# Key-value sums of a linear-attention and expert kernel in five visits instead of nine, with 17 stationary columns, and the placing products in two

## The chip, the core and the metric

The kernel runs on one core of a Trainium2 chip. The metric is the device time of one execution in microseconds (us), and the median of several runs is compared. TensorE is called PE here, and its weight loads PEld; VectorE is DVE, ScalarE is ACT, GpSimd is POOL and SyncE is SP.

## The reference, cut to what matters

A layer norm of `x` (2048 tokens of 512) feeds two branches, and both are added to `x`. The first branch is linear attention with 32 heads of 16: keys and queries go through a small matrix per head and two softmaxes, and the sums over all tokens of key features times values are what the queries are multiplied with. The second is a mixture of eight experts of which each token uses two.

```python
phi_k = concat([softmax(pk), softmax(-pk)])          # 2048 x 32 heads x 32
kv  = einsum("bhsf,bhsd->bhfd", phi_k, v)            # sums over the tokens
z   = einsum("bhsf->bhf", phi_k)
num = einsum("bhqf,bhfd->bhqd", phi_q, kv)
o   = num / (einsum("bhqf,bhf->bhq", phi_q, z)[..., None] + 1e-6)
att = o @ wo
gates = softmax(xn @ wg); top 2 of 8, normalised
out = x + att + sum_e cw[:, e] * (gelu(xn @ w1[e]) @ w2[e])
```

## The kernel before

The 2048 tokens are 16 tiles of 128, in four chunks of four tiles. An opening stretch (to about 162 us) makes the layer norm, the projections and the routing; then eight experts follow, each in 14 steps of 128 hidden columns, 112 steps in all. Nearly every product is taken three times (`mm3`, L174 to L176: high by high, high by low, low by high, of float32r halves), with 128 stationary columns and 496 or 512 moving ones in the opening stretch and 240 to 512 in the experts.

What each function of the opening stretch does, for token tile `t` or chunk `c`:

- `transp(t)` turns the normed tile on PE (L326, four transposes) and splits it: ACT makes the high half (L341), DVE the low half (L342).
- `proj_k(t)`, `proj_v(t)` and `proj_q(c, b)` are the projections, twelve matmuls each. ACT copies the result out (L429 and L430, L361, L479).
- `k_sub(t)` (DVE, L439 to L442), `k_exp(t)` (ACT, L449) and `k_norm(t)` (DVE, L454 to L456) make the key features of a tile in place.
- `kv(t)` (L501) adds a tile's key features times values to a bank of PSUM: 32 float32 matmuls, one for each head, with 18 stationary columns (16 of the values, then two of ones, which POOL fills at L357) and 32 moving columns; head `4b+c` lands in partitions `32c` and up. PE carries each of them out as two records, so that one `kv` is 64 matmul records and 64 weight loads. A tile's feature tile and value tile come free behind it.
- `kv_take(part)` adds a bank's sums to `kb` on DVE (L1080), and `kv_turn` turns them. Of a head's rows only the 16 of the values and the first one of ones (`t[:, :, 16]`) are read later.
- `one_hot(t)` (DVE, L648 and L649) makes two tokens tiles' slot matrices of the routing, and `place(t)` (L658) multiplies them on PE, four float16 matmuls of 144 columns. `route_index` (from L666) reads the sum, and the first expert's tokens are gathered from it.

A visit is a run of one kind of small matmul between the large ones. The order of PE, SP, ACT and DVE is the order of the code: nothing is reordered on these four engines. POOL's instructions are placed by a scheduler. In the opening stretch the `kv` visits stand at L892 (tiles 0 and 1), L901 (2 and 3), L916 (4 and 5) and L1015 (6 and 7). Later work is handed to the experts' steps by a table: `at(s, f, t)` puts `f(t)` behind the first layer and ahead of the second layer of step `s`. There the visits are: tiles 8 and 9 in step 5, 10 and 11 in step 7, 12 and 13 in step 13, 14 in step 20 and 15 in step 21. That makes nine. Memory is handed out by lists (`slot`, `free`), the longest free first in most places, so that another order gives other tiles to the same work.

## Time and profile before

| what | value |
|---|---|
| median of 3 runs | 861.32 us (861.12 to 864.41) |
| the profiled execution's own time | 861.69 us |
| its span, first to last instruction | 859.4 us |
| PE busy | 853.4 us, 99% of the span, 5889 matmul records |
| DVE, ACT and POOL busy | 661.7, 439.1 and 170.7 us |

The page of the profile gives these shares for the whole execution; what single pieces cost is read from the timelines of the engines, which list instructions with their start, duration and number. A matmul's duration there overlaps the next one's, so that the distance from start to start is what counts. `[1.63 <-ACT xTh L341]` behind a row says how long the engine stood idle before it and who ended that.

### The profile page before, as it was taken

What the parts mean: (1) busy time and instruction counts of PE and PEld (TensorE: products, weight loads), DVE (VectorE), ACT (ScalarE), POOL (GpSimd) and SP (SyncE); (2) the same over time, 40 slices, a digit from 0 to 9 for tenths busy, and PEclk for the clock granted to TensorE, in tenths of its full rate; (3) what the DMA queues carried; (4) which work ended last, traced back from release to release, by engine and by line L of the source; (5) the groups of instructions that cost most, each with busy time, mean ns of one, the idle gap of its engine ahead of it and who ended that gap; (6) DMA issues with size and microseconds to landing.
All of it is one profiled execution on the core that took longest, in us unless ns stands there. A gap on an engine that the chain in (4) does not pass through costs nothing.

```text
span 859.4 us, 15983 instructions
## 1 busy us (share of the span) xinstructions
PE 853.4 (99%) x5889; PEld 767.7 (89%) x5889; DVE 661.7 (77%) x1092; ACT 439.1 (51%) x723; POOL 170.7 (20%) x240
## 2 busy tenths in 40 slices
PE   9999999999999999999999999999999999999998
PEld 8888888899999999999999999998877888788886
DVE  6889899888783478878788877978778988755952
ACT  4453522743734364566556665456575566433541
POOL 5000002010004112411241141116421422200011
PEclk9999999999999999999999999999999999999999
DMA  8220106573317341833364257435642735678633
GB/s 296 99 98 2 50 14 191 163 226 100 123 61 223 129 135 47 257 120 110 105 206 134 88 164 191 145 110 165 210 151 83 236 115 187 215 291 248 211 109 101
DMA packets 123399, 126.99 MB, mean 148 GB/s; under 512 B 12342, under 2 KB 87606, under 8 KB 123312
## 3 DMA queue, kind: packets, MB, share of 16 engines
q1 hardware_dynamic: 115408, 106.10, 38.9%
q0 software_dynamic: 7088, 19.36, 7.0%
q8 instruction: 48, 0.79, 0.4%
q10 hardware_dynamic: 816, 0.43, 0.2%
q14 instruction: 39, 0.32, 0.1%
HBM read 98.62 MB, written 27.25 MB: 146 GB/s over the span
## 4 chain that ended last, share of the span: by engine, by line
PE 98%; DVE 1%; DMA 0%; issue 0%; DVEq 0%
PE pH L174 12%; PE pH L175 12%; PE pH L176 12%; PE pY L1259 9%; PE pY L1336 6%; PE pY L1337 6%; PE pY L1342 6%; PE pY L1302 4%; PE pY L1338 2%; PE pY L1339 2%; PE pY L1344 2%; PE pV L174 2%; PE pK L174 2%; PE pQ L474 2%; PE pV L176 2%; PE pO L176 2%
## 5 line engine op out<-in xcount | busy, mean ns | idle before, releaser
L1213 ACT ACTIVATE gl<-pH 128x276 f32<-128x276 f32 (+6 forms) x182 | 77.5, 435 | 242.5 <-PE pH L176 242.3
L1218 DVE TENSOR_TENSOR h<-gl,h 128x512 fp32r<-128x512 f32 (+6 forms) x112 | 78.2, 698 | 98.0 <-ACT h L1215 96.6
L1226 POOL DMA_INDIRECT y_rows<-keptN,pidx x68 | 72.5, 1066 | 235.2 <-ACT gl L1213 200.8
L176 PE MATMUL pH<-keptR,ws 128*128 128x258 f32 (+3 forms) x276 | 82.7, 300 | 0.0
L174 PE MATMUL pH<-keptR,ws 128*128 128x270 f32 (+3 forms) x240 | 72.5, 302 | 0.0
L175 PE MATMUL pH<-keptR,ws 128*128 128x270 f32 (+3 forms) x240 | 72.4, 302 | 0.0
L1215 ACT CAST h<-gl 128x512 fp32r<-128x512 f32 (+6 forms) x112 | 70.5, 629 | 3.5
L175 PE MATMUL pH<-xgl,ws 128*128 128x260 f32 (+3 forms) x204 | 64.6, 317 | 0.0
L174 PE MATMUL pH<-xgh,ws 128*128 128x260 f32 (+3 forms) x204 | 64.6, 316 | 0.0
L1337 PE MATMUL pY<-h,ws 128*128 128x388 f32 (+4 forms) x180 | 62.4, 347 | 0.0
L276 ACT CAST keptR<-keptN 128x1024 fp32r<-128x1024 f32 (+4 forms) x75 | 50.6, 705 | 20.9 <-DVE keptN L996 8.7
L276 ACT CAST ws<-keptN 128x1024 fp32r<-128x1024 f32 x55 | 57.6, 1047 | 7.1 <-PE pY L1259 7.1
L176 PE MATMUL pH<-xgh,ws 128*128 128x272 f32 (+3 forms) x188 | 59.2, 315 | 0.0
L1336 PE MATMUL pY<-h,ws 128*128 128x416 f32 (+4 forms) x168 | 58.5, 348 | 0.0
L1259 PE MATMUL pY<-ws,h 128*128 128x512 f32 x216 | 56.0, 391 | 0.0
L279 DVE TENSOR_TENSOR ws<-keptN,ws 128x1024 fp32r<-128x1024 f32 x36 | 43.5, 1210 | 13.1 <-ACT ws L276 13.0
L176 PEld LDWEIGHTS pH<-keptR,ws 128*128 128x128 f32 x276 | 52.1, 189 | 1.3
L971 POOL DMA_INDIRECT keptN<-xn_rows,tidx x30 | 33.0, 1101 | 97.3 <-DVE vv L675 47.0
L1259 PEld LDWEIGHTS pY<-ws,h 128*128 128x128 f32 x216 | 40.3, 188 | 10.1 <-ACT gl L1213 2.1
L175 PEld LDWEIGHTS pH<-keptR,ws 128*128 128x128 f32 x240 | 45.3, 189 | 2.3
L176 PE MATMUL pH<-xgh,keptR 128*128 128x272 f32 (+3 forms) x148 | 47.1, 318 | 0.0
L174 PEld LDWEIGHTS pH<-keptR,ws 128*128 128x128 f32 x240 | 45.1, 188 | 1.3
(340 smaller groups left out, 2406.0 us busy)
## 6 DMA issues: line engine op xcount, KB each, us to landing
keptN<-in_B_w_dram SPq DMA_DIRECT2D x172, 256.0 KB, 3.8
wr<-in_B_w_dram SPq DMA_DIRECT2D x52, 256.0 KB, 4.1
keptN<-y_rows SPq DMA_DIRECT2D x16, 512.0 KB, 6.0
x_slots<-keptN SPq DMA_DIRECT2D x25, 256.0 KB, 4.7
keptN<-in_A_x_dram SPq DMA_DIRECT2D x16, 256.0 KB, 4.8
xn_rows<-keptN SPq DMA_DIRECT2D x16, 256.0 KB, 2.6
keptN<-x_slots SPq DMA_DIRECT2D x32, 128.0 KB, 4.4
keptN<-in_A_x_dram SPq DMA_DIRECT2D x8, 512.0 KB, 4.5
```

What stands on the lines that cost most here:

```text
L174: nc.tensor.matmul(ps, lh, rh, start=(i == 0), stop=False)
L175: nc.tensor.matmul(ps, lh, rl, start=False, stop=False)
L176: nc.tensor.matmul(ps, ll, rh, start=False, stop=(i == n - 1))
L276: nc.scalar.copy(dst_h, src)
L1213: step[:] = [nc.scalar.activation(g[:, c:c + m], ps[:, :m], AF.Gelu_apprx_tanh)]
L1215: nc.scalar.copy(h[:, 0:full], g)
L1218: nc.vector.tensor_sub(h[:, xw:], g, f32(h[:, 0:full]))
L1226: i = nc.gpsimd.indirect_dma_start(out=to, out_offset=bass.IndirectOffsetOnAxis(ap=rows, axis=0), in_=y, in_offset=None)
L1259: nc.tensor.matmul(yb[e][i], ht[r][:, o:o + P], wsp[r][z][:, D:], start=(b == 0 and low + z == 0), stop=(r % FB == FB - 1 and low > 0))
L1336: nc.tensor.matmul(ps[i][:, 0:w - P], vh, h[:, P:w], start=st, stop=False, skip_group_check=True)
L1337: nc.tensor.matmul(ps[i][:, 0:m], vl, h[:, P:cap], start=False, stop=False, skip_group_check=True)
L1342: nc.tensor.matmul(ps[i][:, 0:m], v[0][:, i * P:(i + 1) * P], h[:, gw + P:], start=False, stop=sp_, skip_group_check=True)
```

## The change

- A `kv` matmul has 17 stationary columns: one column of ones instead of two. `kv_take` reads 17 rows of each head group.
- In the opening stretch `kv(0)` to `kv(3)` are one visit behind `proj_k(8)` to `proj_k(11)`, directly ahead of the transposes of tiles 12 to 15, and `kv(4)` to `kv(7)` are one visit where tiles 6 and 7 were.
- `proj_k(6)` and `proj_k(7)` go ahead of the transposes of tiles 8 to 11, with `k_norm(2)`; `proj_q(0, 3)` goes directly behind the other three of its chunk and ahead of `proj_k(8)`.
- In the experts tiles 8 to 11 are one visit in step 5, and 14 and 15 one visit in step 21. The nine visits become five.
- `place` is called for eight pairs of tiles in two visits of four calls instead of four visits of two.

```diff
-                nc.tensor.matmul(kvp[part][32 * c:32 * c + 18, b * 32:(b + 1) * 32],
-                                 vt[t // 2][:, t % 2, n, :], e[:, n * 32:(n + 1) * 32],
+                nc.tensor.matmul(kvp[part][32 * c:32 * c + 17, b * 32:(b + 1) * 32],
+                                 vt[t // 2][:, t % 2, n, 0:17], e[:, n * 32:(n + 1) * 32],
...
     k_norm(1)
+    proj_k(6)
+    k_norm(2)
+    proj_k(7)
     for t in range(8, 12):
         transp(t)
-    k_norm(2)
-    proj_k(6)
     k_norm(3)
     k_sub(4)
-    proj_k(7)
     k_sub(5)
 
-    for b in range(3):
+    for b in range(4):
         proj_q(0, b)
-    kv(0)
-    kv(1)
     k_exp(4, 5)
...
     k_sub(6)
-    proj_k(8)
-    kv(2)
-    kv(3)
-    proj_k(9)
-    proj_k(10)
-    proj_k(11)
-    proj_q(0, 3)
+    for t in range(8, 12):
+        proj_k(t)
+    for t in range(4):
+        kv(t)
     for t in range(12, 16):
         transp(t)
...
-    kv(4)
-    kv(5)
     proj_k(15)
...
-    kv(6)
-    kv(7)
+    for t in range(4, 8):
+        kv(t)
...
-        if t > 0:
-            place(t - 4)
-            place(t - 2)
+        if t in (8, 16):
+            for u in range(t - 8, t, 2):
+                place(u)
...
-            o, i = (z[32 * c:32 * c + 18] for z in (kb, ps))
+            o, i = (z[32 * c:32 * c + 17] for z in (kb, ps))
...
-        at((t | 1) - 4 if t < 12 else 13 if t < 14 else t + 6, kv, t)
+        at(5 if t < 12 else 13 if t < 14 else 21, kv, t)
```

On PE, the place where tiles 2 and 3 were summed between two key projections before (`pK` is a projection's bank, `kv` the bank of the sums, `pT` one of transposes):

```order
L175 MATMUL pK_1022<-wfl_254,xTh_794 128x496
L176 MATMUL pK_1022<-wfh_253,xTl_796 128x496
L501 MATMUL kv_924<-keptN_80,keptN_86 18x32 x32
L501 MATMUL kv_924<-keptN_84,keptN_86 18x32 x32
L174 MATMUL pK_1102<-wfh_208,xTh_793 128x496
L175 MATMUL pK_1102<-wfl_209,xTh_793 128x496
```

The same sums on PE in the change, behind the projection of tile 11:

```order
L176 MATMUL pK_1018<-wfh_253,xTl_831 128x496
L501 MATMUL kv_1033<-keptN_75,keptN_85 17x32 x32
L501 MATMUL kv_1033<-keptN_76,keptN_85 17x32 x32
L501 MATMUL kv_1033<-keptN_80,keptN_86 17x32 x32
L501 MATMUL kv_1033<-keptN_84,keptN_86 17x32 x32
L326 MATMUL pT_1166<-ident,keptN_78 128x128 x4
L326 MATMUL pT_1175<-ident,keptN_79 128x128 x4
L326 MATMUL pT_1184<-ident,keptN_74 128x128 x4
L326 MATMUL pT_1193<-ident,keptN_82 128x128 x4
L174 MATMUL pK_1217<-wfh_208,xTh_1162 128x496
```

Tiles 0 and 1, which had a visit of their own behind three query projections, and tiles 2 and 3 now stand together, and the transposes follow without a large matmul between.

On PE, behind the first query projection of the second chunk, before:

```order
L475 MATMUL pQ_1380<-keptR_96,wfl_405 128x512
L476 MATMUL pQ_1380<-keptR_98,wfh_404 128x512
L501 MATMUL kv_924<-keptN_76,keptN_89 18x32 x32
L501 MATMUL kv_924<-keptN_80,keptN_89 18x32 x32
L474 MATMUL pQ_1458<-keptR_95,wfh_388 128x512
L475 MATMUL pQ_1458<-keptR_95,wfl_389 128x512
```

and in the change:

```order
L475 MATMUL pQ_1316<-keptR_96,wfl_405 128x512
L476 MATMUL pQ_1316<-keptR_98,wfh_404 128x512
L501 MATMUL kv_1033<-keptN_73,keptN_88 17x32 x32
L501 MATMUL kv_1033<-keptN_71,keptN_88 17x32 x32
L501 MATMUL kv_1033<-keptN_72,keptN_89 17x32 x32
L501 MATMUL kv_1033<-keptN_75,keptN_89 17x32 x32
L474 MATMUL pQ_1458<-keptR_95,wfh_388 128x512
L475 MATMUL pQ_1458<-keptR_95,wfl_389 128x512
```

Tiles 4 and 5 came down from between two key projections; tiles 6 and 7, the last of the four now, stand where they stood.

On ACT, the copies of the query projections and the exponentials of tiles 4 and 5 behind them, as the difference of the two orders:

```order
 L479 COPY keptN_81<-pQ_882 128x512
 L479 COPY keptN_81<-pQ_896 128x512
 L479 COPY keptN_77<-pQ_910 128x512
+L479 COPY keptN_77<-pQ_924 128x512
 L449 ACTIVATE keptN_73<-keptN_73 128x1024
 L449 ACTIVATE keptN_71<-keptN_71 128x1024
```

The fourth query projection's copy now stands ahead of the two exponentials; before it stood behind the copies of tiles 8 to 11.

## Rows read from the trace of the kernel before

**Rows 1.** The page: busy time, share and instructions of each engine, and the shares of the chain that ended last.

```profile
PE 853.4 (99%) x5889; PEld 767.7 (89%) x5889; DVE 661.7 (77%) x1092; ACT 439.1 (51%) x723; POOL 170.7 (20%) x240
PE 98%; DVE 1%; DMA 0%; issue 0%; DVEq 0%
```

**Rows 2.** The waits of PE over the whole span: who waited for whom, us in total, times, longest.

```profile
PE pY L1302 <- DVE h L1218: 0.5, 1, 0.5
```

**Rows 3.** The source view of L501, its two largest groups: duration in ns (min, median, max), first and last start in us, form.

```profile
L501 PEld LDWEIGHTS kv<-keptN,keptN x960: 93/97/99, 73.9 to 295.0; 128*18 128x18 f32 x192
L501 PE MATMUL kv<-keptN,keptN x960: 189/193/206, 73.9 to 295.0; 128*18 128x32 f32 x192
```

**Rows 4.** The timeline of PE around three of the four visits of the opening stretch: start in us, duration in us.

```profile
73.31 0.39 PE L475 MATMUL pQ<-xTh,wfl 128*128 128x512 f32 x1
73.54 0.39 PE L476 MATMUL pQ<-xTl,wfh 128*128 128x512 f32 x1
73.86 1.29 PE L501 MATMUL kv<-keptN,keptN 128*18 128x32 f32 x128
75.08 0.49 PE L174 MATMUL pK<-wfh,xTh 128*128 128x496 f32 x1
75.41 0.39 PE L175 MATMUL pK<-wfl,xTh 128*128 128x496 f32 x1
...
77.96 1.27 PE L501 MATMUL kv<-keptN,keptN 128*18 128x32 f32 x128
79.16 0.49 PE L174 MATMUL pK<-wfh,xTh 128*128 128x496 f32 x1
...
106.75 1.45 PE L501 MATMUL kv<-keptN,keptN 128*18 128x32 f32 x128
108.13 0.50 PE L474 MATMUL pQ<-keptR,wfh 128*128 128x512 f32 x1
```

**Rows 5.** The timeline of PE around two visits in the experts, tiles 8 and 9 at 192.96 and tile 15 at 294.43.

```profile
192.96 1.40 PE L501 MATMUL kv<-keptN,keptN 128*18 128x32 f32 x128
194.29 0.46 PE L1336 MATMUL pY<-h,keptR 128*128 128x424 f32 x1
...
294.08 0.29 PE L175 MATMUL pH<-xgl,keptR 128*128 128x272 f32 x1
294.21 0.29 PE L176 MATMUL pH<-xgh,ws 128*128 128x272 f32 x1
294.43 0.76 PE L501 MATMUL kv<-keptN,keptN 128*18 128x32 f32 x64
295.12 0.45 PE L1336 MATMUL pY<-h,keptR 128*128 128x416 f32 x1
295.41 0.35 PE L1337 MATMUL pY<-h,keptR 128*128 128x416 f32 x1
295.60 0.35 PE L1336 MATMUL pY<-h,keptR 128*128 128x416 f32 x1
```

**Rows 6.** The timelines of PE and DVE: the transposes of tiles 12 to 15, the first low half made from them, and the last instruction of `k_norm(7)`.

```profile
90.06 1.91 PE L326 MATMUL pT<-ident,keptN 128*128 128x128 f32 x16
...
91.15 0.42 DVE L342 TENSOR_TENSOR xTl<-pT,xTh 128x256 fp32r<-128x256 f32 x1 [1.63 <-ACT xTh L341]
...
106.10 1.22 DVE L456 TENSOR_TENSOR keptN<-keptN,sk 128x1024 f32<-128x1024 f32 x1
```

**Rows 7.** The timelines of DVE and ACT around the moved projections: the last low half of tile 11, the copy of the third query projection, the exponential of tile 4 and the first instruction of `k_norm(4)`.

```profile
67.30 0.42 DVE L342 TENSOR_TENSOR xTl<-pT,xTh 128x256 fp32r<-128x256 f32 x1 [0.44 <-ACT xTh L341]
...
74.01 0.59 ACT L479 COPY keptN<-pQ 128x512 f32<-128x512 f32 x1 [2.18 <-PE pQ L476]
76.09 1.06 ACT L449 ACTIVATE keptN<-keptN 128x1024 f32<-128x1024 f32 x1 [1.50 <-DVE keptN L442]
...
78.37 1.21 DVE L454 TENSOR_REDUCE sk<-keptN 128x64 f32<-128x1024 f32 x1
```

**Rows 8.** The timelines of PE and DVE in the placing: the first of the four visits of L658 and what follows it, the last instruction of `one_hot(6)`, and the first read of the sums.

```profile
124.87 0.67 PE L658 MATMUL pI<-oh 128*128 128x144 f16 x8
125.34 0.48 PE L174 MATMUL pV<-keptR,xTh 128*128 128x512 f32 x1
125.66 0.40 PE L175 MATMUL pV<-keptR,xTh 128*128 128x512 f32 x1
...
128.00 0.30 DVE L649 TENSOR_SCALAR keptN<-col,gf,tok 128x144 f16<-128x144 f16 x1
...
135.58 0.31 DVE L666 COPY vv<-pI 128x144 f32<-128x144 f32 x1 [1.03 <-PE pI L658]
```

**Rows 9.** The timeline of DVE in the experts: the last instruction of `k_norm(11)`.

```profile
190.66 1.22 DVE L456 TENSOR_TENSOR keptN<-keptN,sk 128x1024 f32<-128x1024 f32 x1
```

**Rows 10.** The page: the DMA queue that loads PE's program (packets, MB, the time of its packets as a share of 16 engines' span).

```profile
q8 instruction: 48, 0.79, 0.4%
```

**Rows 11.** The DMA view of the stretch from 70 to 80 us: the GB/s in 40 slices of 0.25 us, and the queue of rows 10.

```profile
GB/s 0 0 0 0 0 0 0 0 0 0 0 0 0 0 0 0 0 0 0 0 0 66 0 0 0 0 0 0 0 0 0 0 0 0 0 0 66 0 0 0
...
q8 instruction: 2, 0.03, 1.4%
```

**Rows 12.** The end, where PE leaves the experts' code for code that stands elsewhere: the windows view from 853 us (us, busy time with the number of instructions) and the queue of rows 10 in the DMA view from 853 to 860 us.

```profile
853.00:859.40 6.40, 2.21 (x19) 2.01 (x17) 0.91 (x3) 0.00 (x0) 0.00 (x0) 1.00 0.32 110
...
q8 instruction: 2, 0.03, 2.2%
```

## The prediction

> **What bounds the kernel now.** I read the page first: PE is busy for 853.4 us, 99% of the span, and the chain that ended last lies on PE for 98% [rows 1]. Then PE's waits: behind the start the one that counts is 0.5 us in the experts [rows 2]. So nothing that another engine does faster is worth anything by itself, and a change pays only as far as it shortens PE's own sequence, or as far as PE stays supplied when it comes earlier. Last I read PE's timeline where the diff works. It shows what a visit of small matmuls costs beside its own records [rows 4, 5], and it shows one more thing: the visit at 106.75 takes 1.38 us (to 108.13) for the 128 records that take 1.20 us at 77.96 [rows 4]. Its second half, tile 7, needs `k_norm(7)`, whose last instruction ends at 106.10 + 1.22 = 107.32 [rows 6]. DVE is the slower engine at that point, though no list of waits names it.

> **The fixed price of a visit.** In the opening stretch matmuls of 512 columns start 0.23 apart; the first record of a visit starts 0.32 behind the one ahead of it, and the second matmul behind the visit 0.33 behind the first [rows 4]. That is 0.09 going in and 0.10 coming out. In the experts it is 0.22 against 0.13 and 0.29 against 0.19, the same 0.09 and 0.10 [rows 5]. The body has a fixed part too: 64 records take 0.69 (294.43 to 295.12) and 128 take 1.33 (192.96 to 194.29) [rows 5], so 64 more cost 0.64 and 0.05 is left. A visit thus costs 0.24 us beside its records.

> **Experts, steps 5 and 7, 20 and 21.** Two pairs of visits become two visits: 2 x 0.24 = 0.48 us on PE, all of it on the path. Tile 11 is now wanted two steps earlier, at the end of a visit that began at 192.96; `k_norm(11)` ended at 190.66 + 1.22 = 191.88 [rows 9], so nothing waits. The second layer of step 4 stands 1.3 us later behind the longer visit, and that of step 6 as much earlier; what follows on ACT and DVE moves with PE.

> **Opening stretch, up to the sums of tile 7.** Tiles 0 to 3 in one visit save 0.24, and 0.10 more if the transposes behind them, which are small matmuls themselves, do not pay the way out. The body of 256 records is not in the trace. By half of the 1.20 for each further 64 it takes 2.4, by the 0.575 that is left without the fixed part 2.35, by the experts' 0.64 it takes 2.48, against 1.22 + 1.20 now. So the visit saves between 0.15 and 0.45; I take 0.4, since the first 128 records here ran nearest to the faster end. The transposes of tiles 12 to 15 then start at 89.66 instead of 90.06. DVE stood idle for 1.63 us until they came (91.15) and works without a pause from there to `k_norm(7)` [rows 6], so its end moves by the same 0.4, to 106.92. PE would be at the four sums of tiles 4 to 7 at 106.75 - 0.4 - 1.40 (the visit of tiles 4 and 5, 1.20 + 0.20) = 104.95 and three times 0.58 later, at 106.7, it wants tile 7: it waits some 0.3 us for DVE. Up to here the change is therefore worth what moved the transposes, **0.4 us**; what joining tiles 4 to 7 saves turns into that wait. Behind tile 7 both engines are earlier by the same 0.4, so the routing, whose matmuls follow closely on DVE, keeps its distance.

> **The moved projections.** They remove and add nothing on PE. With `k_norm(2)` ahead of them, the low halves of tiles 8 to 11 end three DVE instructions later, two of them of 1.2 us [rows 6, 7], about 3 us in all: 67.7 [rows 7] becomes 70.7, and the projection that needs them first starts behind 75. The copy of the fourth query projection now stands ahead of `k_exp(4)` on ACT: it comes one projection (12 x 0.23 = 2.7) behind 74.01, ends near 77.3, and `k_exp(4)`, which started at 76.09, ends near 78.4 instead of 77.2 [rows 7]. `k_norm(4)` began at 78.37, so it loses between nothing and 0.1, and the idle 1.63 behind it swallows that [rows 6]. No DMA and no instruction of SP is among what moves; the memory lists give other tiles to the same work, and POOL's fills of ones wait longer for a freed tile, well ahead of the projection that needs them.

> **Placing.** A visit of 8 records takes 0.47 (124.87 to 125.34), and the second matmul behind it comes 0.32 behind the first instead of 0.23 [rows 8]. Nothing shows going in, so a visit costs 0.09 beside its records, and two fewer give **0.18 us**. The first new visit wants `one_hot(6)`, which ended at 128.00 + 0.30 = 128.3 [rows 8] and with the shift ends at 127.9. The visit begins one projection behind where the first one stood, at 124.87 - 0.4 + 2.7 = 127.2, and its last product comes 15 x 0.059 = 0.88 later, so 0.2 is left. DVE waited 1.03 for the last sums [rows 8], so what PE saves is passed on.

> **17 columns.** Loads and matmuls alternate, 9.4 ns for a pair (1.20 / 128) [rows 3, 4]. If the load's columns set that, one of 18 is worth at most 1024 x 9.4 / 18 = 0.5 us; at least nothing. I take nothing, since the same 18 columns run at 9.4 ns here and 10.4 in the experts (1.33 / 128), so something else sets the pace. [...]

> **Loading the program.** Long visits eat code. PE's program comes in 48 packets of 16.5 KB [rows 10], one for about 245 of its 2 x 5889 records [rows 1]: a visit of two tiles is one packet's worth, and a visit of four is two, in 2.2 us. Between 70 and 80 us two packets came, in the slices from 75.25 and from 79.0, just behind the visits; each took 1.4% of 160 us / 2 = 1.1 us [rows 4, 11]. If a packet is asked for when the one ahead of it begins to be used, say in the middle of a visit (74.5), it is there at 75.3 + 1.1 = 76.4, 1.9 us later, while a packet's worth of sums lasts 1.05: 0.85 us of waiting whenever a visit holds two such points. Now the points lie 3.7 us apart and nothing waits. At the end, where PE goes to code elsewhere, two packets come and no more while it runs 36 records [rows 12]; so little is held ahead. The three long visits pay between 0 and 2.55. I take nothing for the first (the transposes and long matmuls behind it give the time), 0.45 for the second (part lies under the wait for DVE) and 0.65 for the third (its records are slower): **1.1 us**, the middle.

> **The sum.** -0.4 - 0.18 - 0.48 = -1.06 (1.1 below), and 1.1 for the loading, which leaves 0.0. The profiled execution's own time is 861.69, 0.37 above the median; against the median of 861.32 the forecast is **861.3 us**, no change. A measurement of this kernel can tell about 0.5% (4.3 us) from no change, and every sum here is smaller.

> **The rivals.**
> 1. The program is held further ahead, and loading costs nothing: -1.1, **860.2 us**. For it: no visit now waits for code, and two packets at the end may be all that was wanted. Against it: the 1.9 us and the 1.05.
> [...]
> 2. The other side: every long visit waits the whole 0.85, because two points fall inside each: 2.55 - 1.1 = +1.45, **862.8 us**. It decides as soon as loading costs more than 1.1 in all. For it: two points must fall somewhere near each visit. [...]
> 3. The column counts: 0.5 less than the forecast, **860.8 us**. Only the equal number of loads and matmuls speaks for it.
> 4. One of the reordered tiles is late in a way I do not see, such as a freed tile that holds a transfer up. The trace has a single wait of PE of 0.5 us among 112 steps [rows 2], so over 4 us is far off.

> **How the numbers follow.** Forecast 0.50, rival 1 0.34, rival 2 0.08, rival 3 0.04, and 0.04 for rival 4 and whatever lies beyond, of which 0.03 is above 865.6. The range takes in rivals 1 to 3 and some spread of the runs, whose lower two lie 0.2 apart: 859.7 to 863.0. Faster by over 0.5% (under 857.0) 0.01, within it 0.96, slower 0.03.

> **What would show it.** Right: the transposes of tiles 12 to 15 start 0.4 earlier; the visit of tiles 4 to 7 shows a pause ahead of tile 7 that ends with `k_norm(7)`; the visit of step 5 lasts more than 2.7 us and holds a pause of PE with no other engine as its cause, with a packet of PE's program landing at its end. If that pause is missing, rival 1 holds. Visits that run below 8 ns for a pair would mean that the 17 columns count. A wait of PE in the experts that was not there, or transposes that do not come earlier, would make the prediction wrong.

## The result: 0.85% slower, where no change was forecast

| | median | runs |
|---|---|---|
| before | 861.77 us | 861.12 to 864.41, 6 runs |
| changed | 869.67 us | 866.82 to 872.52, 6 runs |
| ratio | 1.0085 | 95% interval 1.0066 to 1.0104 |

The forecast was 861.3 us within 859.7 to 863.0. The changed kernel is 8 us slower, above the range. The profiled execution is the fastest of its six (866.82 us, span 864.9); it is 5.1 us above the profiled one of before, and the slowest of the other runs lies 5.7 us higher still. So the trace below accounts for about 5 of the 8 us.

The page of the changed kernel first. To [rows 1] answer the line of PE and that of the chain: PE's busy time is 0.8 us less, but the chain now lies on PE for 94% instead of 98%, and "issue", time in which an engine waited for nothing that the profile shows, has come up to 1%.

```profile
PE 852.6 (99%) x5889; PEld 768.3 (89%) x5889; DVE 662.1 (77%) x1092; ACT 439.0 (51%) x723; POOL 172.3 (20%) x240
PE 94%; DVE 2%; ACT 2%; issue 1%; DMA 0%; DVEq 0%; ACTq 0%
```

The list of PE's waits, the view of [rows 2], names the place: who waited for whom, us in total, times, longest.

```profile
PE kv L501 <- issue: 4.9, 4, 2.4
PE pT L326 <- issue: 0.8, 1, 0.8
PE pY L1295 <- DVE h L1211: 0.5, 1, 0.5
```

The wait for `h` was there before. The other five are new, all stand in or directly behind the joined visits, and no engine is named as their cause. PE's timeline shows them (start, duration, then idle time and who ended it in brackets); [rows 4 to 6] show the same places before.

```profile
86.55 2.54 PE L501 MATMUL kv<-keptN,keptN 128*17 128x32 f32 x256
89.02 1.31 PE L326 MATMUL pT<-ident,keptN 128*128 128x128 f32 x10
91.12 0.87 PE L326 MATMUL pT<-ident,keptN 128*128 128x128 f32 x6 [0.79 <-issue]
91.75 0.47 PE L174 MATMUL pK<-wfh,xTh 128*128 128x496 f32 x1
...
105.41 1.82 PE L501 MATMUL kv<-keptN,keptN 128*17 128x32 f32 x189
109.61 0.85 PE L501 MATMUL kv<-keptN,keptN 128*17 128x32 f32 x67 [2.38 <-issue]
110.38 0.50 PE L474 MATMUL pQ<-keptR,wfh 128*128 128x512 f32 x1
...
194.98 2.51 PE L501 MATMUL kv<-keptN,keptN 128*17 128x32 f32 x227
199.24 0.42 PE L501 MATMUL kv<-keptN,keptN 128*17 128x32 f32 x29 [1.75 <-issue]
199.59 0.46 PE L1329 MATMUL pY<-h,keptR 128*128 128x424 f32 x1
...
297.28 0.96 PE L501 MATMUL kv<-keptN,keptN 128*17 128x32 f32 x80
298.62 0.27 PE L501 MATMUL kv<-keptN,keptN 128*17 128x32 f32 x4 [0.38 <-issue]
299.33 0.68 PE L501 MATMUL kv<-keptN,keptN 128*17 128x32 f32 x44 [0.44 <-issue]
299.93 0.45 PE L1329 MATMUL pY<-h,keptR 128*128 128x416 f32 x1
```

Before, the projection behind the same transposes, and the first transposes of the kernel before and after:

```profile
91.72 0.47 PE L174 MATMUL pK<-wfh,xTh 128*128 128x496 f32 x1
...
9.68 0.60 PE L326 MATMUL pT<-ident,keptN 128*128 128x128 f32 x4
...
9.20 0.60 PE L326 MATMUL pT<-ident,keptN 128*128 128x128 f32 x4
```

Read the starts, since durations overlap. The transposes take 2.73 us to the projection behind them instead of 1.66 (90.06 [rows 6] to 91.72); the visit of tiles 4 to 7 takes 4.97 us, that of 8 to 11 takes 4.61, that of 14 and 15 takes 2.65. Undisturbed the three visits take 2.38 (run `aligned` below), some 2.65 (an estimate, twice the 1.33 of [rows 5]) and 1.38 (run `behind`). That is 1.07 + 2.59 + 1.96 + 1.27 = 6.9 us lost in five pauses. The matmul behind the last visit starts only 4.8 us later than before (299.93, and 295.12 in [rows 5]), so 2.1 us were gained up to there: 0.5 lies ahead of the change (the first transposes start at 9.20 instead of 9.68), and the rest, 1.6, stands beside the 1.06 that the forecast had.

In the visit of tiles 4 to 7 the DMA view of 105.4 to 110.4 us (GB/s in 40 slices of 0.125 us, a packet counted in the slice in which it starts; q8 loads PE's program [rows 10], the 66 is another queue's) shows one packet of PE's program.

```profile
GB/s 0 0 0 0 0 0 0 0 0 0 0 131 0 0 0 0 0 0 0 66 0 0 0 0 0 0 0 0 0 0 0 0 0 0 0 0 0 0 0 0
...
q8 instruction: 1, 0.02, 1.8%
```

It starts in the slice from 106.78, 1.4 us into the visit, and takes 1.8% of 16 times 5 us, 1.4 us, to 108.2 or 108.3. PE has done its 189th matmul by 107.23 (105.41 + 1.82) and goes on at 109.61, another 1.3 us behind the packet's end. The prediction had such a pause, of at most 0.85 us; this one is nearly three times as long.

The three pauses ahead of tiles 14 and 15 also stand where packets meet. The windows view from the end of the pause in the transposes to that in the visit of tiles 4 to 7, and from there to that in the visit of tiles 8 to 11 (us; busy time of PE, PEld, DVE, ACT and POOL with the number of instructions in brackets; PE's granted clock as a share of full speed, DMA share, GB/s):

```profile
91.10:109.60 18.50, 16.11 (x255) 13.52 (x255) 16.26 (x30) 8.08 (x19) 0.22 (x1) 1.00 0.01 2
109.60:199.20 89.60, 87.88 (x761) 77.19 (x761) 75.65 (x204) 35.95 (x59) 10.29 (x11) 1.00 0.50 148
```

Between them lie 255 and 761 matmuls with as many loads, and the trace has 2 and 14 other instructions of PE there (semaphores, registers, a branch): 512 and 1536 instructions, two and six times 256. The two pauses of tiles 14 and 15 do not fit this count.

### The profile page after: what moved, and what is told of

The parts are those of the page before. It is cut to its first block, busy times and chain, and to the rows that moved or that the text cites. A ratio compares the mean times of both kernels' runs of the same rounds, so it can differ in the third digit from the quotient of the medians.

```text
span 864.9 us, 15980 instructions
## 1 busy us (share of the span) xinstructions
PE 852.6 (99%) x5889; PEld 768.3 (89%) x5889; DVE 662.1 (77%) x1092; ACT 439.0 (51%) x723; POOL 172.3 (20%) x240
## 3 DMA queue, kind: packets, MB, share of 16 engines
q1 hardware_dynamic: 115408, 106.10, 38.5%
## 4 chain that ended last, share of the span: by engine, by line
PE 94%; DVE 2%; ACT 2%; issue 1%; DMA 0%; DVEq 0%; ACTq 0%
PE pH L174 12%; PE pH L175 12%; PE pH L176 11%; PE pY L1252 9%; PE pY L1329 6%; PE pY L1330 6%; PE pY L1335 6%; PE pY L1295 2%; PE pY L1331 2%; PE pY L1332 2%; PE pY L1337 2%; PE pV L174 2%; PE pQ L474 2%; PE pV L176 2%; PE pO L176 2%; PE pO L174 2%
## 5 line engine op out<-in xcount | busy, mean ns | idle before, releaser
L1211 DVE TENSOR_TENSOR h<-gl,h 128x512 fp32r<-128x512 f32 (+6 forms) x112 | 78.4, 700 | 99.9 <-ACT h L1208 78.7
```

What stands on the lines that cost most here:

```text
L1211: nc.vector.tensor_sub(h[:, xw:], g, f32(h[:, 0:full]))
```

## The experiments

The theory: PE waits for its own program whenever a visit uses up more than one packet's worth (256 instructions, 128 matmuls with their loads, by the counts above) in a microsecond or so. The rivals: the new order of the projections, the placing visits or the 17 columns bring the loss; or a visit of four tiles waits for data.

**after_again**, the changed kernel once more.

> The changed kernel once more, for the spread of its runs and a second profile. Loading theory (TensorE waits for its own program whenever more than one packet's worth of instructions, some 256, is used up in a microsecond or so): the same pauses of PE with no engine as their cause, behind the same instructions: about 1.0 us in the transposes behind the first visit, 2.5 in the visit of tiles 4 to 7, 1.9 in that of tiles 8 to 11; the time 866 to 872 us. The two pauses of 0.6 us in the visit of tiles 14 and 15, which lie at no packet's edge, may be missing. Rival (the pauses come from a neighbour that happens to be late, such as a transfer): they stand elsewhere or differ by more than 0.5 us. If the granted clock is below 1 in this profile, the windows show where.

Measured: 867.48 us median (866.14 to 869.68), ratio 1.0083 [1.0069, 1.0097]. The waits stand where they stood: 2.37 us in the visit of tiles 4 to 7 (behind its 189th matmul again), 1.7 in that of 8 to 11, 0.75 in the transposes. The pauses of tiles 14 and 15 are weaker, the visit takes 1.86 us. This profile has something that the first one lacks. The windows view behind the visit of tiles 4 to 7, where the granted clock is the third number from the end:

```profile
109.50:110.50 1.00, 1.00 (x66) 0.91 (x54) 0.90 (x4) 0.00 (x0) 0.21 (x1) 1.00 0.06 16
110.50:112.50 2.00, 2.00 (x6) 1.58 (x6) 1.76 (x8) 0.00 (x0) 0.00 (x0) 0.52 0.00 0
112.50:114.00 1.50, 1.50 (x5) 1.12 (x5) 1.04 (x6) 0.00 (x0) 0.00 (x0) 0.50 0.00 0
114.00:115.00 1.00, 1.00 (x6) 0.83 (x5) 0.00 (x0) 0.39 (x1) 0.00 (x0) 0.99 0.00 0
```

The granted clock is 0.50 for some 3.4 us, and matmuls of 512 columns start 0.43 apart instead of 0.23: nine of them, from 110.55 to 114.19, take 3.64 us instead of 2.1, so the fall costs 1.6. It came some 1.4 us after PE had taken up work again (at 109.20). In the first profile the clock stayed at 1.00 behind the same pause (109.6 to 114 us).

**pairs**, the nine visits restored, all else kept.

```diff
...
-    for t in range(4, 8):
-        kv(t)
+    kv(6)
+    kv(7)
...
-        at(5 if t < 12 else 13 if t < 14 else 21, kv, t)
+        at((t | 1) - 4 if t < 12 else 13 if t < 14 else t + 6, kv, t)
```

> The changed kernel with the sums back in nine visits; the 17 columns, the order of the projections and the two placing visits stay. Loading theory: no pause is left, 860.7 to 861.5 us, some 0.2 under the kernel before. Rival (the new order, the placing or the 17 columns bring the loss): 866 us or more.

Measured: 860.38 us beside 860.71 before, ratio 0.9995 [0.9986, 1.0003]. No pause without a cause is left in PE's list. The order of the projections, the placing in two visits and the 17 columns cost nothing. The columns do not count either way: the pair of tiles 2 and 3, with 17 columns and between the same neighbours, takes 1.19 us (79.56 to 80.75), against 1.20 [rows 4].

**joined**, the kernel before with the visits joined and nothing else (the lines of the single visits go).

```diff
...
     proj_q(0, 3)
+    for t in range(4):
+        kv(t)
     for t in range(12, 16):
...
-        at((t | 1) - 4 if t < 12 else 13 if t < 14 else t + 6, kv, t)
+        at(5 if t < 12 else 13 if t < 14 else 21, kv, t)
```

> The kernel before with the visits joined as in the change (five in place of nine, the first behind the fourth query projection) and nothing else: 18 columns, placing in four, projections in the old order. Loading theory: pauses of 1 to 2.6 us with each visit of four tiles, 866 to 870 us. Rival (order, placing or columns): 860.5 to 861.5 us.

Measured: 868.97 us, ratio 1.0093 [1.0078, 1.0107]. Joining the visits alone brings the whole loss. Its list of waits:

```profile
PE kv L501 <- issue: 4.0, 2, 2.1
PE pT L326 <- DVE xTl L342: 1.8, 1, 1.8
```

The third wait, in the transposes, names DVE; the weight load of the same matmul has stood idle for 2.04 us with "issue" as the cause. Which of the two ended it is not told apart here.

The granted clock fell to 0.50 twice in this profile, at about 110.8 and 203.0 us, each time within 1.1 us of PE's going on behind a pause in a joined visit, and for some 3.4 us.

**half**, 16-bit operands: a matmul is one record instead of two (5377 matmul records of PE on the page, and 5889 in the changed kernel), so that a visit of four tiles has one packet's worth.

```diff
-            vt[t // 2] = slot([P, 2, 32, 18], name="v", keep=t >= 8)
+            vs[t // 2] = slot([P, 2 * 32 * 18], name="v", keep=t >= 8)
+            vt[t // 2] = vs[t // 2].bitcast(F16)[:, 0:2 * 32 * 18].rearrange("p (y b j) -> p y b j", y=2, b=32)
...
-        e = ekt.rearrange("p h s j -> p (h s j)")
+        e = ekt.rearrange("p h s j -> p (h s j)").bitcast(F16)[:, 0:1024]
...
```

> The changed kernel with keys and values of the sums in 16 bit (float16), so that the operands are rounded and a matmul takes one record in place of two, and a weight load too: a visit of four tiles has 256 records instead of 512, one packet's worth. Loading theory: no pause in any visit, and if the number of records sets the pace, visits of half the length: 855.5 to 858 us; if the columns set it, up to 860.5. Rival (a visit of four tiles waits for something else, order or data): the pauses stay, 864 us or more.

Measured: 855.95 us, ratio 0.9941 [0.9928, 0.9954]. The timeline of the first two visits of four tiles:

```profile
86.79 1.23 PE L504 MATMUL kv<-keptN,keptN 128*17 128x32 f16 x128
...
103.32 0.94 PE L504 MATMUL kv<-keptN,keptN 128*17 128x32 f16 x96
105.45 0.37 PE L504 MATMUL kv<-keptN,keptN 128*17 128x32 f16 x32 [1.19 <-DVE keptN L459]
```

Four tiles take the time that two took (1.16 us for the first visit), and no pause is without a cause. So four tiles in one visit are not the trouble, nor their data; the number of instructions is. The page also gives the size of a packet: q8 has 44 instead of 48 with 1024 matmuls and loads fewer, 256 for each. The one wait in a visit is the one that the prediction named: tile 7 waits for `k_norm(7)` (L459 here).

**half_late**, that visit one projection later (the diff is against `half`).

```diff
-    for t in range(4, 8):
-        kv(t)
     proj_q(1, 1)
+    for t in range(4, 8):
+        kv(t)
```

> The 16-bit kernel of the first set with the visit of tiles 4 to 7 one projection later, behind the second of the two around it (operands of the sums rounded, as there). In that kernel PE waits 1.3 us in this visit for DVE's last normalized key; the projection, which takes 2.8 us, covers it. Expected: no such wait, 854.3 to 855.0 us instead of 856.0. Rival (the routing that follows on DVE then comes later and PE waits there instead): 855.5 to 856.5.

Measured: 856.01 us, ratio 0.9943 [0.9929, 0.9958]: nothing gained, the rival was right. The wait in the visit is gone, and PE's list has 1.0 us for `pR L580 <- DVE cum` and 0.4 for `pR L579 <- DVE m` instead: the routing behind it hangs on the same DVE work.

**aligned**, work added to move the points at which a packet ends.

```diff
     proj_k(12)
+    for _ in range(93):
+        nc.tensor.ldweights(idle[:, 0:1])
     proj_k(13)
...
     split_x(0, 0, 1)
+    for _ in range(77):
+        nc.tensor.ldweights(idle[:, 0:1])
     proj_q(3, 2)
```

> The changed kernel with work added: 93 weight loads of one column (nothing reads them) behind the first projection of the last chunk's keys, ahead of the visit of tiles 4 to 7, and 77 more ahead of the visit of tiles 8 to 11. They shift the places at which a packet of PE's program ends: in these two visits from 378 and 454 instructions behind the visit's start to 285 and 284, so that the packet needed there is asked for before the visit begins, among long matmuls, and the one behind it is needed only among the long matmuls that follow (541 and 540). Loading theory: the pauses of 2.5 and 1.9 us are gone, the one of 0.9 us in the transposes (first visit, not shifted) stays; 861.0 to 864 us, by what 170 loads cost (between 5 and 25 ns each, 0.8 to 4 us). Rival (the pause comes with a visit of four tiles wherever the packet ends): both pauses stay, 867 us or more.

Measured: 866.55 us, ratio 1.0063 [1.0047, 1.0078]: above the 861.0 to 864 that were expected and close to the rival's 867, but the trace answers the question. PE's timeline of the two visits:

```profile
106.75 2.46 PE L501 MATMUL kv<-keptN,keptN 128*17 128x32 f32 x256
109.13 0.50 PE L474 MATMUL pQ<-keptR,wfh 128*128 128x512 f32 x1
...
194.57 1.57 PE L501 MATMUL kv<-keptN,keptN 128*17 128x32 f32 x142
196.96 1.28 PE L501 MATMUL kv<-keptN,keptN 128*17 128x32 f32 x114 [0.82 <-issue]
198.16 0.46 PE L1333 MATMUL pY<-h,keptR 128*128 128x424 f32 x1
```

The same 256 matmuls of tiles 4 to 7 run through in 2.38 us. The DMA view from 104.5 to 109.5 us (slices of 0.125 us) shows why: a packet of q8 starts in the slice from 105.13, before the visit; without the added loads it starts 1.4 us into it.

```profile
GB/s 0 0 0 0 0 131 0 0 0 0 0 0 0 0 0 0 0 0 0 0 0 0 0 0 0 0 0 66 0 0 0 0 0 0 0 0 131 0 0 0
...
q8 instruction: 2, 0.03, 2.6%
```

In the visit of tiles 8 to 11 the pause moved from behind the 227th matmul to behind the 142nd, as computed (284 instructions), and shrank from 1.75 to 0.82 us; the first layer's matmuls ahead of it start 0.13 apart instead of 0.23, which leaves less time (argued, not varied). The total was missed for other reasons: the pauses in the transposes (0.9) and in the visit of tiles 14 and 15 stayed, the added loads took some 1.9 us, and one wait for DVE at 628 us grew from 0.5 to 1.9; it is as long in `wide`, and its cause stays open.

**double**, each matmul of tiles 8 to 11 issued twice (they count double in the sums).

```diff
-                nc.tensor.matmul(kvp[part][32 * c:32 * c + 17, b * 32:(b + 1) * 32],
+                for i in range(2 if part == 1 else 1):
+                    nc.tensor.matmul(kvp[part][32 * c:32 * c + 17, b * 32:(b + 1) * 32],
...
```

> The changed kernel with each matmul of the visit of tiles 8 to 11 issued twice (these tiles count double in the sums): 1024 instructions in one visit. Loading theory (some 3.6 us from asking for a packet to its first instruction, against 1.3 us that its 256 instructions last): pauses of 1.9, 2.3 and 2.3 us at 454, 710 and 966 instructions; the visit takes 11.5 to 12.5 us instead of 4.6, and the kernel 873 to 878 us. Rival (one wait in each visit, of fixed size): one pause, a visit of 7.3 us, 868.5 to 873.

Measured: 875.53 us, ratio 1.0164 [1.0145, 1.0182]. PE's timeline of the visit:

```profile
196.10 2.47 PE L502 MATMUL kv<-keptN,keptN 128*17 128x32 f32 x227
200.95 1.59 PE L502 MATMUL kv<-keptN,keptN 128*17 128x32 f32 x128 [2.37 <-issue]
204.50 1.96 PE L502 MATMUL kv<-keptN,keptN 128*17 128x32 f32 x128 [1.97 <-issue]
207.96 0.64 PE L502 MATMUL kv<-keptN,keptN 128*17 128x32 f32 x29 [1.50 <-issue]
208.53 0.72 PE L1330 MATMUL pY<-h,keptR 128*128 128x424 f32 x1
```

This is the clearest row of the study. PE stops behind every 128 matmuls, which with their loads are 256 instructions, and from one stop's end to the next 3.55 and 3.46 us go by. That is what a packet costs when loading sets the pace. The granted clock is 0.50 here from 202.2 us on; the matmuls became slower, and the pauses shorter by about as much. The DMA view of 201 to 206 us (slices of 0.125 us; the values from 203.5 to 205.1 are another queue's) shows how the 3.5 us are made up:

```profile
GB/s 16 33 16 0 0 0 0 0 0 131 0 0 0 0 0 0 0 0 0 0 4 86 111 94 152 254 315 344 307 238 135 49 8 0 0 0 131 0 0 0
...
q8 instruction: 2, 0.03, 2.3%
```

The packets start in the slices from 202.13 and from 205.50 and take 0.92 us each (2.3% of 16 times 5 us, by two). PE had gone on at 200.95, so 1.2 us pass until the first starts; it ends at about 203.1, and PE goes on at 204.50, another 1.4 us later. The second ends at about 206.5, and PE goes on at 207.96.

**wide**, 64 moving columns instead of 32: as many instructions, each longer.

```diff
-                nc.tensor.matmul(kvp[part][32 * c:32 * c + 17, b * 32:(b + 1) * 32],
-                                 vt[t // 2][:, t % 2, n, 0:17], e[:, n * 32:(n + 1) * 32],
+                nc.tensor.matmul(kvp[part][32 * c:32 * c + 17, b * 64:(b + 1) * 64],
+                                 vt[t // 2][:, t % 2, n, 0:17], e[:, None, n * 32:(n + 1) * 32].to_broadcast([P, 2, 32]),
...
```

> The changed kernel with matmuls of 64 columns in place of 32 in all visits (each moving operand read twice, the second result unused): the same number of instructions, each up to twice as long. Loading theory: where the program is late, slower instructions fill the time of the pause; the visits of tiles 4 to 7 and 8 to 11 grow by less than half of what their sums grow (if a sum takes 1.6 times as long, each pause shrinks by about 1 us and the visits take 5.0 to 5.8 us instead of 5.0 and 4.6), while the visit of tiles 12 and 13, where nothing waits, shows the whole growth (from 1.35 to 2.0 us or more). Rival (the pause is a wait of fixed size, whatever the engine does in between): pauses of the same length as in the changed kernel, and all visits grow in proportion.

Measured: 868.56 us, ratio 1.0084 [1.0065, 1.0102], as slow as the changed kernel (1.0085); the profiled execution is the slowest of the five (872.74). Two tiles where nothing waits (12 and 13) go from 1.35 to 1.91 us, and the first visit from 2.47 to 3.70, with the pause in the transposes behind it down from 0.79 to 0.2. The visit of tiles 4 to 7 goes from 4.97 to 5.33 only, its wait from 2.38 to 1.33: slower instructions filled the pause. The visit of tiles 8 to 11 did not follow: 6.27 us, its wait grew from 1.75 to 2.29. Why is open. Its length alone says little: behind the same 227 matmuls as in the changed kernel the wait was 1.75, 1.7 and, in `double`, 2.37 us. So the first two places bear the theory out here, and the third decides nothing.

**last20, last21, swapped and behind** are about the two pauses of tiles 14 and 15, which lie 8 instructions apart and stayed behind the 80th matmul when `aligned` shifted the program by 170. All four start from pairs. The diff is that of last20; last21 has 21 there, swapped has tiles 12 and 13 at step 21 and tiles 14 and 15 at 20, and behind calls `kv(14)`, `kv(15)` and `kv_take(2)` after `layer2` of step 21.

```diff
-        at((t | 1) - 4 if t < 12 else 13 if t < 14 else t + 6, kv, t)
+        at((t | 1) - 4 if t < 12 else 13 if t < 14 else 20, kv, t)
```

> The changed kernel with pairs of tiles in each visit (as in the run with nine visits), only that the single visits of tiles 14 and 15 become one, at step 20. In the changed kernel that visit stood at step 21 and paused twice for 0.6 us while POOL's indirect DMA of the block before ran; at step 20 none of it lies beside the visit in the trace. Theory (PE's instructions come late while POOL issues an indirect DMA; 256 instructions alone are no harm): no pause, the visit 1.35 us, 859.9 to 860.4 us against 860.7 before, as the pairs less one visit's 0.24. Rival (256 instructions in this place pause by themselves): two pauses, 861 us or more.

> The same with the joined visit of tiles 14 and 15 at step 21, where the changed kernel has it, all other visits being pairs. Theory (POOL's indirect DMA beside the visit): the visit takes 1.9 to 2.7 us instead of 1.35, with pauses while POOL's instruction runs; 860.4 to 861.5 us, 0.6 to 1.3 above the run with step 20. Rival (the pauses of the changed kernel come from the program being late behind its longer visits): no pause, the visit 1.35 us, the same time as at step 20.

> The same with tiles 14 and 15 at step 20 and the visit of tiles 12 and 13, which stood at step 13 and never paused, at step 21 instead. Theory (POOL's indirect DMA beside the visit): the pauses move to tiles 12 and 13, whose visit takes 1.9 to 2.7 us; that of 14 and 15 takes 1.35. Rival (something of tiles 14 and 15 themselves): tiles 12 and 13 take 1.35 us in their new place.

Measured: last20 861.37 us, ratio 1.0003 [0.9994, 1.0013]; last21 861.56, 1.0009 [1.0000, 1.0018]; swapped 862.77, 1.0017 [1.0008, 1.0025]. All the joined visits paused, at step 20 as at step 21, and tiles 12 and 13 too when they stood there (2.63 us, after 1.35 at step 13). The expectation for step 20 was wrong in its premise: an indirect DMA of POOL runs there too. It starts some 0.8 us behind the visit's start; a visit of one tile, 0.69 us, is over before, a visit of two is not. The timelines of PE and POOL in last20:

```profile
286.63 0.94 PE L501 MATMUL kv<-keptN,keptN 128*17 128x32 f32 x83
287.99 0.26 PE L501 MATMUL kv<-keptN,keptN 128*17 128x32 f32 x5 [0.42 <-issue]
288.72 0.61 PE L501 MATMUL kv<-keptN,keptN 128*17 128x32 f32 x40 [0.47 <-issue]
289.26 0.46 PE L1335 MATMUL pY<-h,ws 128*128 128x416 f32 x1
...
287.41 0.97 POOL L1225 DMA_INDIRECT y_rows<-keptN,pidx  x1 [4.99 <-ACT gl L1212]
```

PE's first pause opens about when POOL starts, and the second closes some 0.3 us after POOL is done.

> As the run with the joined visit of tiles 14 and 15 at step 21, all other visits being pairs, only that this visit stands behind the step's second layer instead of ahead of it, some 3 us later, where POOL's indirect DMA (about 1 us, from 0.8 us behind the visit's former start) is over. Theory (the pauses come from POOL's indirect DMA beside the visit): no pause, the visit 1.35 us; 860.0 to 860.6 us, under the kernel before by about 0.3 and under the run at step 21 by 1.3 in the visit. Rival (256 instructions of these two tiles pause by themselves, wherever they stand): the visit takes 1.9 to 2.7 us here too.

```profile
295.08 1.45 PE L501 MATMUL kv<-keptN,keptN 128*17 128x32 f32 x128
296.46 0.39 PE L174 MATMUL pH<-xgh,keptR 128*128 128x272 f32 x1
...
292.92 0.97 POOL L1225 DMA_INDIRECT y_rows<-keptN,pidx  x1 [4.99 <-ACT gl L1212]
```

Measured: 860.49 us beside 861.39, ratio 0.9995 [0.9985, 1.0006]. With POOL's instruction over at 293.89 the visit takes 1.38 us without a pause. Its neighbours on PE are others here, too. That POOL's instruction is the cause rests on this run and on the visits that had it beside them; by what way it acts is open.

## Why the prediction was wrong

- **The step that failed: "Loading the program", the term of 1.1 us.** The mechanism was there, its size was not. The estimate had a packet usable when its transfer ends, 1.9 us after it is asked for, and took that request to fall where the packet ahead begins to be used (an estimate: no view shows the request); 0.85 us were then left for each visit, 2.55 at most in three. Where loading alone sets the pace, 3.5 us go by for each packet (`double`): 1.2 until the transfer starts, 0.9 for the transfer, and 1.4 from its end to PE's next instruction (1.3 in the visit of tiles 4 to 7). That last wait the prediction put at nothing, without a row for it. Against 1.2 to 1.3 us of sums for 256 instructions (the prediction's 1.05 follows from no row: 128 pairs take 1.20 in [rows 4]) up to 2.4 us are left in a visit. The three places lost 1.07, 2.59 and 1.96, together 5.6 us, where the prediction had nothing, 0.45 and 0.65. In its sum, 5.6 in place of 1.1 gives -1.06 + 5.6 = +4.5.
- **The packets at [rows 11 and 12] could not show it.** What they hold is the transfer (1.1 us). The time behind it shows only where PE runs out of instructions, and in no visit before it did: a pair is one packet's worth, with long matmuls on both sides.
- **Rival 2 had the right sign and place** (a full wait in every visit, 862.8) and the same wrong price; 2.55 was called the most that loading could cost, which made the range too narrow at the top. Rival 1 was to hold if the pause in the visit of step 5 was missing; it is there, 1.75 us in a visit of 4.61.
- **"Experts", tiles 14 and 15:** a collision that was not thought of, 1.27 us in the profiled execution. The step's "nothing waits" was about the data of tile 11 alone.
- **The clock** had no term. Means of 0.995 to 0.999 in the six runs stand beside 872.5 to 866.8 us, while the eleven runs of pairs have 0.999 and 1.000. A second profile shows one fall, worth 1.6 us, behind a pause; the profiles without pauses show none before the end (0.99 or more in every window up to 852 us). One fall goes with a mean of 0.998 (`after_again`) and two with 0.996 (`joined`), so by an estimate the six runs hold from none to about three, up to 5 us; that could be a good part of what their median has beyond the profiled run. Every fall before the end stands behind a pause, but not every pause is followed by one (`after`, `wide`). That the pauses bring it on is argued and not shown: no run changed the clock alone.
- **What held:** the fixed price of a visit (1.6 us gained beside the pauses, against 1.06), the transposes that come earlier (by 1.04, of which 0.5 was there from the start, against 0.4), 17 columns at nothing, placing and moved projections at no cost (`pairs`).
- **What did not show:** the wait for `k_norm(7)` in the visit of tiles 4 to 7. DVE came earlier with the transposes, as forecast, and ends at 105.08 + 1.22 = 106.30 (the row below); PE, held up in the transposes, would be at tile 7 only at about 107.2. So the joined visit kept its saving, part of the 1.6. The wait is there in `half` (1.19), where no pause holds PE up and the visits are shorter.

```profile
105.08 1.22 DVE L456 TENSOR_TENSOR keptN<-keptN,sk 128x1024 f32<-128x1024 f32 x1
```

## What to carry to other kernels

Count instructions, not only busy time: here runs of tiny matmuls of more than 256 instructions with their loads were paced by the loading of PE's program (3.5 us for each 256 in `double`, which take 1.2 to 1.3 us where nothing waits). Whether a run of 512 pauses hangs on where the packets meet in it: one ran through in `aligned` (2.38 us). So runs of small matmuls are better cut into pieces of that size with long matmuls between them (`pairs`, 0.9995 instead of 1.0085), or made with fewer instructions, as 16-bit operands did (0.9941 with rounded sums). In the traces here this showed as idle time of PE with "issue" as its cause, a multiple of 256 instructions apart (512 and 1536 in the changed kernel, 256 in `double`). And no wait seen before is no proof of a margin: ask what kept it away, here the long matmuls between the pairs.

Neither joined visits nor the other edits gave a float32 version that is measurably faster than before; pairs and behind both measure 0.9995, with intervals that hold 1.
